# Convolution and MLP block in FP32: fewer idle matmuls ahead of the first group, another split of the last group, one statistics chain for the first two

One core of a Trainium2 chip. The metric is the device time of one execution in microseconds (us), median of several; "slow" states are told apart, and all runs quoted here are of the fast state. The trace and the page come from one profiled execution of each kernel. Its span is 1.7 to 2.0 us shorter than its time. "Clock" is the share of TensorE's full clock that the record shows as granted, as a mean over a run unless a stretch is named.

## The reference

```python
# x: (8, 4224, 192) f32, weight: (8 heads, 7 taps)
w   = softmax(weight, axis=-1)                     # per head
x   = causal depthwise conv over the sequence: sum_k w[h, k] * x_pad[:, s + k, head h]
mu  = mean(x, -1);  var = mean((x - mu)**2, -1)    # moe block, D = 192
xn  = (x - mu) / sqrt(var + 1e-6) * g_ln
out = x + relu(xn @ w_ch1) @ w_ch2                 # 192 -> 768 -> 192
```

## The kernel before

The work is cut into 18 groups of (128 partitions x n tokens), n = 6, 8, 9, 10 for the first sequence and then 16 and 17 by turns; the last is group 17 with 17 tokens. For each group VectorE convolves (`conv`), transposes (`yt`) and takes statistics; TensorE does the up product (`ph`, ScalarE's Relu empties it from PSUM), then the down product, which is either plain (`po`) or made of seven half products instead of eight (`pd`, Strassen's scheme, 7/8 of the columns for some additions on VectorE). The last group does 9 tokens the fast way and 8 the plain way, in two pieces of 4. Cut to what the change touches:

```python
fast = {g: groups[g][2] if g >= 5 else 0 for g in range(NG)}   # tokens by half products
fast[NG - 1] = (J + 1) // 2                                    # J = 17: 9 in the last group
psum = ctx.enter_context(tc.tile_pool(name="ps", bufs=8, space=PSUM))
...
def keep_warm(times):                       # matmuls whose result nobody reads
    idle = psum.tile([P, 512], F32, tag="ps", name="idle")
    for _ in range(times):
        nc.tensor.matmul(idle[:, 0:P], less, copy, start=True, stop=True)
...
def blocks(n):
    half = n if n * C <= 512 else (n + 1) // 2                 # C = 32 columns a token
    return [slice(i, min(i + half, n)) for i in range(0, n, half)]
...
# up(g): for each of 6 chunks f and each block: four PSUM banks, 6 x 4 matmuls, four Relus
# down(g): for each c: one bank, 6 x 4 matmuls
    order = [(c, js) for c in range(NC) for js in blocks(n)]
    if g + 1 == NG:
        order = [(c, slice(j, j + 4)) for j in range(fast[g], n, 4) for c in range(NC)]
...
keep_warm(20)
first_tap(0, heads=(0, PE_HEADS[0])); conv(0, heads=PE_HEADS[0])
centre_w1()                                 # needs the first weights, loaded by DMA
keep_warm(24)
first_tap(1); transpose(0)                  # VectorE: input of group 0
split_words(*words_2); join_words(w2flat, *words_2)   # w2: VectorE and ScalarE (L189)
for g in range(NG):
    up(g)
    ...
    if g < 4: stats(g)                      # bn_stats per token, then 16 small operations
    ...
    if fast[g]: finish_fast(g, *parts)      # additions, 6 transposes
    if g + 1 == NG: add_and_store(g, slice(0, fast[g]))
    down(g); finish(g)                      # per bank a transpose; adds; last store
```

## Time and profile before

| | before |
|---|---|
| median, first 3 runs | 1017.43 us (1017.35 to 1017.55) |
| span of the profiled run | 1015.5 us |
| TensorE busy | 1004.1 us (99%) |
| VectorE busy | 899.1 us (89%) |
| ScalarE busy | 491.9 us (48%) |

TensorE is busy without a hole from the first product of group 0 to the last group, so only the two ends and the number of columns can give anything. The lines that show this, and how to read them, are in the prediction below. PE is TensorE, PEld its weight loads, DVE VectorE, ACT ScalarE; "<-" ahead of a name says what ended an idle time.

### The profile page before, as it was taken

To read this page: it belongs to the slowest core of one execution; us is meant where nothing else is said; L and a number is where in the kernel's file an instruction comes from. 1 tells how busy PE (TensorE), PEld (TensorE's weight loads), DVE (VectorE), ACT (ScalarE), POOL (GpSimd) and SP (SyncE) were. 2 spreads that over 40 slices of the span, in tenths; PEclk is the share of its full clock that TensorE was granted. 3 is DMA by queue.
4 is the path that set the end of the run, shared out by engine and by line. 5 is a ranking of instruction groups with operands and counts; after the bars stand their busy time and mean duration, and the time that the engine had idled before them with its cause. 6 is when DMAs were issued, how large, how long until landed. Compare 5 with 4: busy or idle time off the path is not lost.

```text
span 1015.5 us, 35457 instructions
## 1 busy us (share of the span) xinstructions
PE 1004.1 (99%) x15940; PEld 657.0 (65%) x15940; DVE 899.1 (89%) x1791; ACT 491.9 (48%) x1306; POOL 41.1 (4%) x59
## 2 busy tenths in 40 slices
PE   7999999999999999999999999999999999999997
PEld 6987564348545785458754686556854578545897
DVE  7999798955999999999998999989999999999535
ACT  6445344406445464555536465364644546453450
POOL 1001000000000000000000000000000000000000
PEclk9999999999999999999999999999999999999999
DMA  5233541502323433123333331334232343112031
GB/s 195 100 125 103 160 130 56 161 35 39 89 92 63 157 65 149 34 45 150 64 149 51 117 90 34 148 68 157 39 88 93 64 157 64 65 32 37 2 66 69
DMA packets 12214, 91.45 MB, mean 90 GB/s; under 512 B 1695, under 2 KB 2463, under 8 KB 8222
## 3 DMA queue, kind: packets, MB, share of 16 engines
q1 hardware_dynamic: 6862, 64.91, 16.6%
q0 software_dynamic: 4896, 24.28, 14.3%
q8 instruction: 124, 2.03, 0.8%
q14 instruction: 28, 0.23, 0.1%
q10 hardware_dynamic: 304, 0.00, 0.0%
HBM read 38.95 MB, written 50.23 MB: 88 GB/s over the span
## 4 chain that ended last, share of the span: by engine, by line
PE 98%; DVE 1%; DMA 0%; ACT 0%; issue 0%; DVEq 0%; ACTq 0%
PE ph L444 51%; PE pd L542 35%; PE po L480 11%; PE idle L313 1%; DMA taps<-in_weight_dram 0%; PE pc L273 0%; PE pw L297 0%; PE pw L302 0%; ACT room L266 0%; DVE y L622 0%; PE pm L282 0%; PE pm L285 0%; DVE room L205 0%; DVE room L197 0%; DVE room L194 0%
## 5 line engine op out<-in xcount | busy, mean ns | idle before, releaser
L444 PE MATMUL ph<-yt,w 32*128 32x256 f32 (+4 forms) x7200 | 516.5, 443 | 0.0
L444 PEld LDWEIGHTS ph<-yt,w 32*128 32x128 f32 x7200 | 364.3, 185 | 149.7 <-issue 117.5
L346 DVE SCALAR_TENSOR_TENSOR y<-xg,taps,y 128x384 f32<-128x384 f32 (+5 forms) x852 | 429.1, 582 | 0.0
L456 ACT ACTIVATE ht<-ph 128x288 f32<-128x288 f32 (+4 forms) x600 | 222.7, 457 | 265.7 <-PE ph L444 262.7
L542 PE MATMUL pd<-ht,w 128*32 128x256 f32 (+2 forms) x2808 | 155.9, 378 | 0.0
L542 PE MATMUL pd<-ht,w2sums 128*32 128x256 f32 (+2 forms) x2808 | 153.2, 378 | 0.0
L542 PEld LDWEIGHTS pd<-ht,w 128*32 128x32 f32 x2808 | 89.5, 110 | 64.6 <-issue 6.9
L542 PEld LDWEIGHTS pd<-ht,w2sums 128*32 128x32 f32 x2808 | 90.9, 110 | 59.9
L480 PE MATMUL po<-ht,w 128*32 128x128 f32 (+5 forms) x2016 | 112.5, 383 | 1.2 <-issue 1.2
L547 ACT COPY cs<-pd 128x272 f32<-128x272 f32 (+2 forms) x156 | 58.3, 373 | 109.1 <-PE pd L542 109.1
L509 DVE TENSOR_TENSOR s<-ht 128x1088 f32<-128x1088 f32 (+2 forms) x39 | 47.5, 1219 | 56.8 <-ACT ht L456 56.8
L480 PEld LDWEIGHTS po<-ht,w 128*32 128x32 f32 x2016 | 62.1, 110 | 50.7 <-issue 23.8
L610 ACT ACTIVATE ot<-ot,r 128x192 f32<-128x192 f32 x247 | 93.1, 471 | 0.0
L547 ACT COPY part<-pd 128x272 f32<-128x272 f32 (+2 forms) x117 | 43.5, 372 | 86.2 <-PE pd L542 86.2
L336 ACT ACTIVATE y<-xg,taps 128x384 f32<-128x384 f32 (+5 forms) x142 | 74.1, 591 | 22.7 <-DVE st L370 18.3
L370 DVE BATCH_NORM_STATS2 st<-y 128x6 f32<-128x192 f32 x264 | 69.7, 341 | 0.0
L357 DVE STREAM_TRANSPOSE yt<-y 128x3072 f32<-128x3072 f32 (+5 forms) x18 | 56.0, 3111 | 1.7 <-DVE y L346 1.0
L614 POOL DMA_DIRECT2D out_dram<-ot x34 | 29.5, 883 | 664.6 <-DVE y L346 388.3
L542 PE MATMUL pd<-s,w2sums 128*32 128x272 f32 (+2 forms) x936 | 52.6, 378 | 0.0
L510 DVE TENSOR_TENSOR ht<-ht 128x1088 f32<-128x1088 f32 (+2 forms) x39 | 47.6, 1220 | 2.2
L586 DVE STREAM_TRANSPOSE ot<-cs 128x544 f32<-128x544 f32 (+2 forms) x78 | 47.5, 672 | 0.0
L520 DVE TENSOR_TENSOR ht<-s,ht 128x1088 f32<-128x1088 f32 (+2 forms) x39 | 45.2, 1214 | 1.6 <-PE pd L542 1.6
(76 smaller groups left out, 280.7 us busy)
## 6 DMA issues: line engine op xcount, KB each, us to landing
xg<-in_x_dram SPq DMA_DIRECT2D x7, 2208.0 KB, 12.5
out_dram<-ot POOLq DMA_DIRECT2D x20, 768.0 KB, 6.7
xg<-in_x_dram SPq DMA_DIRECT2D x7, 2112.0 KB, 11.8
out_dram<-y SPq DMA_DIRECT2D x7, 1536.0 KB, 6.0
out_dram<-y SPq DMA_DIRECT2D x6, 1632.0 KB, 6.2
out_dram<-ot POOLq DMA_DIRECT2D x6, 864.0 KB, 7.5
out_dram<-y SPq DMA_DIRECT2D x2, 864.0 KB, 4.2
xg<-in_x_dram SPq DMA_DIRECT2D x1, 1536.0 KB, 8.8
```

Of the source, the lines that this page charges most:

```text
L336: nc.scalar.mul(dst, src, tap)
L346: nc.vector.scalar_tensor_tensor(out=y[g][:, 0:n, cs], in0=t[:, k : k + n, cs], scalar=taps[:, h, k : k + 1], in1=y[g][:, 0:n, cs], op0=AL ...
L357: nc.vector.transpose(yt[g][:, 0:n].rearrange("p j c t -> p (j c t)"), y[g][:, 0:n].rearrange("p j d -> p (j d)"),)
L370: nc.vector.bn_stats(out=st[:, j, :], in_=y[g][:, j, :])
L444: nc.tensor.matmul(ph[q][:, 0:w], w1[rows, c, fs], t[rows, js, c, :], start=(c == 0), stop=(c == NC - 1),)
L456: nc.scalar.activation(dst, src, AF.Relu)
L480: nc.tensor.matmul(bank[C * q : C * q + C, 0:w], w2[:, f, C * c : C * c + C], t[:, f, q, js.start - fast[g] : js.stop - fast[g], :], start ...
L509: nc.vector.tensor_tensor(s1[g][:, f], a[:, 1, 0, f], a[:, 1, 1, f], op=ALU.add)
L510: nc.vector.tensor_tensor(a[:, 1, 0, f], a[:, 0, 0, f], a[:, 1, 0, f], op=ALU.subtract)
L542: nc.tensor.matmul(dst[C * q : C * q + C, 0:w], right[:, f, C * c : C * c + C], left[:, f, q], start=(first and f == 0), stop=(f == FC - 1 ...
L547: nc.scalar.copy(to[:, c], dst[:, 0:w].rearrange("p (j t) -> p j t", t=T))
L610: nc.scalar.mul(ots[g][:, j, :], ots[g][:, j, :], rstd[g][:, j : j + 1])
```

## The change

The intent: let group 0 start sooner, move three tokens of the last group from the plain product to the cheaper half products, finish the last group with fewer instructions and in one piece, and save VectorE one chain of small operations. Core of the diff:

```diff
-    fast[NG - 1] = (J + 1) // 2
+    fast[NG - 1] = J - 5
@@ stats: split into moments(g) (bn_stats) and root(g, n) (the chain)
+        if g == 0:
+            moments(0)
+        elif g == 1:
+            moments(1)
+            root(0, groups[0][2] + groups[1][2])
+            rstd[1] = rstd[0][:, groups[0][2] :]
@@ blocks
-        half = n if n * C <= 512 else (n + 1) // 2
-        return [slice(i, min(i + half, n)) for i in range(0, n, half)]
+        cut = fast[g] if 0 < fast[g] < n else n // 2 if n * C > 512 else 0
+        return [slice(0, cut), slice(cut, n)] if cut else [slice(0, n)]
@@ down
-            order = [(c, slice(j, j + 4)) for j in range(fast[g], n, 4) for c in range(NC)]
+            order = [(c, slice(fast[g], n)) for c in range(NC)]
@@ down_fast, two half products before its end; finish_fast now takes one half
+        if g + 1 == NG:
+            finish_fast(g, 0, cs, part)
@@ head
-    keep_warm(24)
+    keep_warm(12)
```

More of the change, by code (lines that the diff above doesn't have):

```diff
@@ L360, in transpose, with moments, root @@
         )
+    sums = {}
+    def moments(g):
+        n = groups[g][2]
+        if g == 1:
+            sums[g] = sums[0][:, groups[0][2] :]
+        else:
+            sums[g] = spool.tile([P, J, nc.vector.BN_STATS_DIM], F32, tag="st", name=f"st{g}")
+        for j in range(n):
+            nc.vector.bn_stats(out=sums[g][:, j, :], in_=y[g][:, j, :])
     def stats(g):
-        n = groups[g][2]
-        st = spool.tile([P, J, nc.vector.BN_STATS_DIM], F32, tag="st", name=f"st{g}")
+        moments(g)
+        root(g, groups[g][2])
+    def root(g, n):
+        st = sums[g]
         dt = spool.tile([P, J], F32, tag="d", name=f"d{g}")
@@ L368, in stats @@
         d, v, r = dt[:, 0:n], vt[:, 0:n], rt[:, 0:n]
-        for j in range(n):
-            nc.vector.bn_stats(out=st[:, j, :], in_=y[g][:, j, :])
         nc.vector.tensor_tensor(d, st[:, 0:n, 1], st[:, 0:n, 4], op=ALU.subtract)
@@ L407, with blocks @@
     ht = {}
-    def blocks(n):
-        half = n if n * C <= 512 else (n + 1) // 2
-        return [slice(i, min(i + half, n)) for i in range(0, n, half)]
+    def blocks(g):
+        n = groups[g][2]
+        cut = fast[g] if 0 < fast[g] < n else n // 2 if n * C > 512 else 0
+        return [slice(0, cut), slice(cut, n)] if cut else [slice(0, n)]
     def up(g):
@@ L434, in up @@
             fs = slice(f * P, f * P + P)
-            for js in blocks(n):
+            for js in blocks(g):
                 w = (js.stop - js.start) * C
@@ L471, in down @@
         po[g] = []
-        order = [(c, js) for c in range(NC) for js in blocks(n)]
+        order = [(c, js) for c in range(NC) for js in blocks(g)]
         if g + 1 == NG:
-            order = [(c, slice(j, j + 4)) for j in range(fast[g], n, 4) for c in range(NC)]
+            order = [(c, slice(fast[g], n)) for c in range(NC)]
         for c, js in order:
@@ L577, in down_fast, with finish_fast @@
         return cs, part
-    def finish_fast(g, cs, part):
+    def finish_fast(g, half, cs, part):
         n = fast[g]
-        ot = out_tile(g)
-        c21, c22 = cs[:, 0:CH, :, 1], cs[:, CH:NC, :, 1]
-        nc.vector.tensor_tensor(c21, c21, part[:, 1], op=ALU.add)
-        nc.vector.tensor_tensor(c22, c22, part[:, 2], op=ALU.add)
-        for c in range(NC):
+        ot = ots[g] if half else out_tile(g)
+        fresh = cs[:, CH * half : CH * half + CH, :, 1]
+        nc.vector.tensor_tensor(fresh, fresh, part[:, 1 + half], op=ALU.add)
+        for c in range(CH * half, CH * half + CH):
             nc.vector.transpose(
@@ L684 @@
                 store_y(g + 1)
-        if g < 4:
+        if g == 0:
[4 more added lines that the diff above has]
+            rstd[1] = rstd[0][:, groups[0][2] :]
+        elif g < 4:
             stats(g)
@@ L690 @@
         if fast[g]:
-            finish_fast(g, *parts)
+            for half in range(g + 1 == NG, 2):
+                finish_fast(g, half, *parts)
         if g + 1 == NG:
```

## The prediction

> **What bounds the kernel now.** I read the page first, for the bound, then the waits of TensorE, then the two ends in the timeline and in the chain that ended last, because the middle turned out to have no hole in it.
>
> The page's busy row, and its chain by engine:
>
> ```profile
> PE 1004.1 (99%) x15940; PEld 657.0 (65%) x15940; DVE 899.1 (89%) x1791; ACT 491.9 (48%) x1306; POOL 41.1 (4%) x59
> ...
> PE 98%; DVE 1%; DMA 0%; ACT 0%; issue 0%; DVEq 0%; ACTq 0%
> ```
>
> The matrix engine is the bound: 98% of the path that sets the end is its work. The waits of that engine alone (who waited on whom, us in total, times, longest):
>
> ```profile
> PE idle L313 <- POOL room L251: 4.8, 1, 4.8
> PE po L480 <- issue: 1.2, 2, 0.9
> PE pm L282 <- DVE room L205: 0.9, 1, 0.9
> ```
>
> It waits at the very start, and for 1.2 us "issue" in the last down product. From the first product of group 0 (28.86 us) to there it never waits. So a change counts only in three ways: fewer or cheaper TensorE instructions, an earlier start of group 0, or a shorter tail. The start of group 0, in the timeline (start, length, engine, what):
>
> ```profile
> 23.31 5.62 PE L313 MATMUL idle<-room 128*128 128x128 f32 x48
> ...
> 25.69 1.38 DVE L357 STREAM_TRANSPOSE yt<-y 128x1152 f32<-128x1152 f32 x1 [0.51 <-DVE y L346]
> ...
> 28.86 11.98 PE L444 MATMUL ph<-yt,w 32*128 32x192 f32 x288
> ...
> 29.21 1.26 ACT L189 ACTIVATE spare<-spare,low 128x1152 int32<-128x1152 int32 x1 [0.30 <-DVE spare L186]
> ...
> 31.16 1.00 ACT L456 ACTIVATE ht<-ph 128x192 f32<-128x192 f32 x4 [0.69 <-PE ph L444]
> ```
>
> The input of group 0 is transposed at 25.69 + 1.38 = 27.07 us, but the idle matmuls (24 in the program, 48 records, two passes each) hold the engine until 28.86. The tail, in the chain in order of time:
>
> ```profile
> 977.88 15.57 PE pd L542 x504
> 993.45 8.94 PE po L480 x326
> 1002.39 0.88 issue
> 1003.27 3.70 PE po L480 x128
> 1006.97 0.32 issue
> 1007.30 2.38 PE po L480 x77
> ...
> 1012.00 0.33 DVE y L622 x2
> ```
>
> The last group ends with 15.57 us of half products (9 tokens), 17.5 us of plain product (8 tokens, two pieces), then transposes, adds and a store.
>
> **What the Trainium skill says.** "TensorE: Matmul & The Clock Gate", section "Back-to-back issue gap", gives a warm matmul N/2.4 + 2.5 ns. The trace agrees if an FP32 pass counts two cycles a column: 63 sets of four 256-column matmuls took 27.33 us, 433.8 ns a set, two passes of 216.9; the formula at N = 512 gives 215.8. "ScalarE: Activation LUTs", section "What ACT_TABLE_LOAD costs", gives an ACTIVATE 0.833 ns per element; here four Relus of 256 columns take 1.21 us and of 288 columns 1.32 us in the timeline, 0.86 ns a column. "Runtime: NRT & Kernel Launch", section "Instruction fetch mechanics", says an engine's instructions come in blocks of 256 (16 KiB), fetched by DMA and mostly hidden. The trace agrees on the size (the instruction queue has 124 packets in 2.03 MB; between the two "issue" gaps lie 128 matmul and 128 weight-load records) and shows two that are not hidden, while the tail's stores run. The first page's section "Why this matters for your kernels" asks for no idle gap over about 3 us; the change leaves one of 1 us, and the page shows full clock in every slice, although the engine already sits idle for 0.88 us at L282. So I expect no clock loss.
>
> **The change part by part.**
>
> *Idle matmuls, 24 to 12.* 48 records took 23.31 to 28.86, 0.1156 us each. With 24 the engine is free at about 26.1 and then waits for the transposed input, 27.07 + 0.05 (the lag seen from DVE L205's end, 12.30, to the product at 12.35). Group 0 starts at 27.12: 1.74 us earlier. But something takes part back. Eight PSUM banks hold two blocks of four, so the third block needs the first Relus done. ScalarE's queue holds the conversion of w2 (L189) before them; it ends at 30.47 whatever TensorE does, because it waits for VectorE. The first four Relus then end near 31.6 rather than follow the product at 29.4. The third block would start at 27.12 + 2 x 1.985 = 31.1, so about 0.5 us of wait, with weight load 0.6. Net **-1.15 us**. The input of group 1 is ready at 49.09 + 1.78 = 50.87; the product would want it at 52.61 - 1.15 = 51.46, so no wait, but only 0.6 us to spare.
>
> *One statistics chain for groups 0 and 1.* Removes 16 VectorE operations at about 0.18 us spacing, 2.9 us in all (52.44 to 55.36). VectorE is not on the path there: group 2's input is ready at 74.9, used at 84.1. **0 us.**
>
> *Middle groups.* The block cut of the 17-token groups becomes 8 + 9 instead of 9 + 8: the same columns. The order of instructions on each engine shows no other move. **0 us.**
>
> *Last group, up products.* Two blocks of 288 and 256 columns become 384 and 160; the sum is equal, so are the matmul counts. But the 160-column block lasts only 6 sets x 274 ns = 1.64 us, and within it four Relus of 384 columns have to free the banks that the next block takes: 1.32 + 4 x 96 x 0.00086 = 1.65 us, after a lag of 0.3 us (the Relu starts 0.3 us after the next block's first matmul in the trace), plus the last one's overlap. The fourth bank comes free some 0.35 us late, 0.55 with the weight load. There are five such hand-overs. If each costs in full it is 1.75 us or more; if the row groups can run a little apart, a part is absorbed. I take **+1.1 us**.
>
> *Last group, down.* A half product of w columns: 144 columns take 15.57/63 = 247.1 ns a set, 256 take 433.8, so 192 take 327.1 and 63 sets 20.61 us: +5.04. The plain piece: 128 columns take 219 ns a set (banks are released every 1.31 us, six sets), so 160 take 274 and 36 sets 9.86 us, instead of 72 x 219 = 15.78: -5.92. Sum **-0.88 us**. This is the intended saving (three more tokens at 7/8 of the plain cost).
>
> *The fetch gaps.* The engine's end was about 1010.98 = 993.45 + 15.78 + 1.75, so gaps with restart cost 1.75 us, though the waits show 1.2. After the change the plain piece has half the instructions, so a block of 256 lasts 4.4 us instead of 3.5. The program has 48 + 576 = 624 TensorE instructions fewer, which puts the last two block edges 388 and 132 instructions from the end, 6.6 and 2.3 us before it. The big store starts about 4.7 us before the end, so those blocks should be on their way by then. **-1.75 us**, the least certain gain.
>
> *The tail after TensorE.* Half of the fast result is now finished while two half products still run. VectorE's remaining three transposes, then 12 adds at 0.339 us (9 took 3.05), end some 4.7 us before TensorE ends, in time for the plain banks. After the fifth bank come 5 wide adds instead of 4 and 5 narrow ones: 1.55 us behind TensorE instead of 1.35, **+0.2**. The last store is 480 KB instead of 384: from 2.3 us for 384 KB and 4.1 for 864, **+0.36**.
>
> Sum: -1.15 + 1.1 - 0.88 - 1.75 + 0.56 = **-2.1 us**: 1017.43 becomes about 1015.3; I put it at 1015.1, because I think the hand-over more likely smaller than larger.
>
> **The rivals.**
>
> *A. The hand-over wait eats the gain.* Each of the five costs 0.55 us or more and they add up to nearly 3 us, or a fetch gap stays. For it: ScalarE alone releases those banks, with 1.65 us of work in 1.64. Against: four banks are released one by one, three of them in time. It would end at 1016.5 to 1017.5.
>
> *B. All parts go well.* Group 0 starts 1.74 us earlier with nothing taken back, the fetch gaps vanish, the hand-over costs nothing: 1.74 + 0.88 + 1.75 - 0.56 = 3.8, 1013.6. Against: L189's end is fixed by VectorE.
>
> *C. The earlier start is lost later.* VectorE, 89% busy, becomes the limit for some group's input, and the head's gain is waited away there. For it: the 0.6 us to spare at group 1. Against: in the later groups VectorE's work hangs on TensorE's own progress, and before group 17 the input is ready at 942.1, used at 944.6. It would cost 1.15: 1016.3.
>
> *D. VectorE becomes the tail*, with 12 adds and wider transposes. I find 1 us of slack; if a late ScalarE copy uses it up, the end moves by under 1 us.
>
> **Range and chances.** Head -0.7 to -1.74, hand-over 0 to +2.5, fetch -0.5 to -1.75, the rest firm to some 0.3. Not all go one way, so 1013.4 to 1016.8 holds it 8 times in 10. Two per cent is 20 us; the whole of both ends that the change touches is smaller than that, except by a fault. Within 2%: 0.985.
>
> **What would show it.** Right: the idle group has 24 records, group 0 starts near 27.1; a wait of about 0.5 us on ScalarE in its third block; five waits or stretched blocks in the last up stage (33.25 us becomes about 34.3); half products of 20.6 us, plain ones of 9.9 without an "issue" gap; VectorE's last add 1.5 us behind the last product. Wrong: a clock under 1.00 after the gap, an "issue" gap in the plain piece, a wait of TensorE on VectorE at group 1 or 2, or the twelve adds running into the plain banks.

## The result, and the profile after

1014.28 us (1014.06 to 1014.6, 6 runs) against 1017.49 us (1017.35 to 1017.69, 6 runs) of the kernel before on the same chip: ratio 0.9969, 95% interval 0.9956 to 0.9981. Ratios are the mean time of one kernel's fast runs over that of the other's of the same rounds, so not quite the ratio of the medians quoted. The gain is 3.2 us; the prediction's sum had 2.1 and its number 2.3, and the time lies inside its range.

TensorE's waits after, all of them (us in total, times, longest):

```profile
PE idle L313 <- POOL room L251: 4.8, 1, 4.8
PE ph L457 <- DVE yt L357: 1.0, 1, 1.0
PE pm L282 <- DVE room L205: 0.6, 1, 0.6
```

The "issue" wait of the last down product is gone, and there is a new wait of 1.0 us: group 0 now waits for its transposed input and no longer for the idle matmuls. The timeline of the head after the change:

```profile
23.26 2.94 PE L313 MATMUL idle<-room 128*128 128x128 f32 x24
...
25.64 1.38 DVE L357 STREAM_TRANSPOSE yt<-y 128x1152 f32<-128x1152 f32 x1 [0.51 <-DVE y L346]
...
27.16 12.25 PE L457 MATMUL ph<-yt,w 32*128 32x192 f32 x288 [0.96 <-DVE yt L357]
...
29.16 1.26 ACT L189 ACTIVATE spare<-spare,low 128x1152 int32<-128x1152 int32 x1 [0.30 <-DVE spare L186]
30.32 2.01 ACT L469 ACTIVATE ht<-ph 128x192 f32<-128x192 f32 x8
```

The first Relus start when L189 is done, eight in one run with no wait between: that is the part given back. The product of group 0 is listed with 12.25 us against 11.98. And the tail, in the chain that ended last. The up stage of group 17 before:

```profile
944.66 33.21 PE ph L444 x576
```

and all of it after:

```profile
943.23 33.60 PE ph L457 x558
976.83 20.61 PE pd L555 x504
997.44 8.19 PE po L493 x240
...
1008.32 0.49 DVE y L636 x3
```

The stages of both kernels, from the records in the two traces (from the first matmul of a stage to the first of the next; the plain stage to its last matmul):

| us | before | after | difference | predicted |
|---|---|---|---|---|
| first matmul of group 0 | 28.86 | 27.16 | -1.70 | -1.74 |
| its up stage | 11.91 | 12.18 | +0.27 | +0.6 |
| all from there to group 17 | 903.82 | 903.82 | 0 | 0 |
| up stage of group 17 | 33.21 | 33.60 | +0.39 | +1.1 |
| half products | 15.46 | 20.50 | +5.04 | +5.04 |
| plain product | 17.44 | 9.66 | -7.78 | -7.67 |
| last matmul to last add | 1.62 | 1.89 | +0.27 | +0.2 |
| last add to the span's end | 3.21 | 3.49 | +0.28 | +0.36 |
| sum | | | -3.23 | -2.1 |

The sum is the difference of the spans, 1015.54 and 1012.29, to the rounding. The whole middle, 904 us with 17 groups, is the same to 10 ns.

### The profile page after: what moved, and what is told of

Same layout as the page of the kernel before. It is cut to its first block, busy times and chain, and to the rows that moved or that the text cites. A ratio compares the mean times of both kernels' runs of the same rounds, so it can differ in the third digit from the quotient of the medians.

```text
span 1012.3 us, 34807 instructions
## 1 busy us (share of the span) xinstructions
PE 1000.9 (99%) x15628; PEld 648.8 (64%) x15628; DVE 900.4 (89%) x1766; ACT 490.5 (48%) x1306; POOL 41.1 (4%) x59
## 4 chain that ended last, share of the span: by engine, by line
PE 97%; DVE 2%; DMA 0%; ACT 0%; issue 0%; DVEq 0%; ACTq 0%
PE ph L457 51%; PE pd L555 35%; PE po L493 10%; DVE y L346 1%; DMA taps<-in_weight_dram 0%; DVE y L636 0%; ACT room L266 0%; DVE room L197 0%; DVE yt L357 0%; DVE room L194 0%; ACT room L181 0%; DVE ot L653 0%; ACT room L189 0%; DVE room L186 0%; DVE room L180 0%
## 5 line engine op out<-in xcount | busy, mean ns | idle before, releaser
L457 PE MATMUL ph<-yt,w 32*128 32x256 f32 (+6 forms) x7200 | 517.1, 443 | 1.0 <-DVE yt L357 1.0
L469 ACT ACTIVATE ht<-ph 128x256 f32<-128x256 f32 (+6 forms) x600 | 222.7, 457 | 268.9 <-PE ph L457 265.5
L555 PE MATMUL pd<-ht,w 128*32 128x256 f32 (+2 forms) x2808 | 158.0, 382 | 0.0
L555 PE MATMUL pd<-ht,w2sums 128*32 128x256 f32 (+2 forms) x2808 | 155.3, 381 | 0.0
L493 PE MATMUL po<-ht,w 128*32 128x192 f32 (+5 forms) x1728 | 106.0, 406 | 0.0
L493 PEld LDWEIGHTS po<-ht,w 128*32 128x32 f32 x1728 | 55.6, 110 | 49.5 <-issue 22.1
L600 DVE STREAM_TRANSPOSE ot<-cs 128x544 f32<-128x544 f32 (+2 forms) x78 | 50.0, 690 | 2.7 <-ACT cs L560 1.0
```

The source lines that it names most:

```text
L457: nc.tensor.matmul(ph[q][:, 0:w], w1[rows, c, fs], t[rows, js, c, :], start=(c == 0), stop=(c == NC - 1),)
L469: nc.scalar.activation(dst, src, AF.Relu)
L493: nc.tensor.matmul(bank[C * q : C * q + C, 0:w], w2[:, f, C * c : C * c + C], t[:, f, q, js.start - fast[g] : js.stop - fast[g], :], start ...
L555: nc.tensor.matmul(dst[C * q : C * q + C, 0:w], right[:, f, C * c : C * c + C], left[:, f, q], start=(first and f == 0), stop=(f == FC - 1 ...
L600: nc.vector.transpose(ot[:, 0:n, C * c : C * c + C], cs[:, c].rearrange("p j h t -> p j (h t)"))
```

## The experiments

They ran on three other chips, in three lots of four. There the first weights arrive later: the first real matmul (`pm`) starts at 14.2 to 14.5 us instead of 12.3, and the kernel before takes about 1020 us. Many of their runs also show a mean clock of 0.994 to 0.998 instead of 0.999 or 1.000. So beside the medians I give the median of the runs with a clock of 0.999 and above, called "full clock": it compares like with like. For the kernel before this is 1019.93 us on the chip of the first lot (32 of 47 runs), 1019.81 on that of the second (28 of 41) and 1019.52 on that of the third (6 of 14).

### 1. Idle matmuls back to 24

```diff
-    keep_warm(12)
+    keep_warm(24)
```

> The changed kernel with its 12 idle matmuls set back to 24, nothing else. Theory (the idle matmuls held back group 0, and ScalarE's conversion of w2 gives back about 0.35 us): group 0 starts near 28.9 us instead of 27.16, its up stage takes 11.9 us again instead of 12.25, and the time is 1.4 us above the changed kernel, about 1015.7. Rival (an earlier start is lost later, or the whole gain is the tail's): less than 0.4 us above it.

Median 1018.43 us; ratio to before 0.9983 (0.9976 to 0.999). At full clock 1018.34 (14 runs), 1.6 below the kernel before; experiment 4, which has the 12 idle matmuls, is at 1016.25. The head is worth 2.1 us on this chip, not 1.4. In the traces group 0 starts at 31.57 us here and at 29.14 in experiment 8, another chip with the weights as late, and its up stage takes 11.91 against 12.18: 2.43 - 0.27 = 2.16. The mechanism is the one expected; the size depends on when the weights come. The idle matmuls start after the weights' work (26.02 us here, 23.31 on the first chip) but the input of group 0 is ready only 2.0 us later than there (29.07 against 27.07), so 24 of them overrun it by more.

### 2. No idle matmuls ahead of group 0

```diff
-    keep_warm(12)
```

> The changed kernel with no idle matmul ahead of group 0. Theory (after the change the start of group 0 is set by VectorE's transposition, which ends at 27.03 us): group 0 starts at 27.1 to 27.2 again and the time is the changed kernel's, 1014.3 give or take 0.3. Rival (the clock gate closes in the 3.9 us without a matmul[...]): the first products of group 0 take up to twice as long, the recorded clock is lower, and the time is 1.5 to 3 us longer.

Median 1017.72 us (11 runs), none at full clock: 0.995 to 0.998. That is 1.5 us above experiment 4 at full clock. The rival is right. The stretch of group 0's up stage (columns: length, then busy us and count of PE, PEld, DVE, ACT and POOL, the granted clock, the DMA share, GB/s), and the next:

```profile
27.00:42.83 15.83, 13.66 (x293) 13.22 (x296) 14.10 (x29) 11.48 (x35) 0.00 (x0) 0.89 0.37 134
42.83:48.00 5.17, 5.17 (x131) 4.13 (x135) 5.17 (x17) 1.64 (x6) 0.00 (x0) 1.00 0.02 3
```

A mean of 0.89 over 15.83 us is 3.5 us at half clock. The record has one such stretch of 3.41 us here (and one earlier), and the up stage of group 0 took 13.35 us instead of 12.18. That stretch began at 28.96 us, within a wait of 2.2 us ahead of group 0. So the idle matmuls do a job, and 12 are not just "fewer is better".

### 3. The last group's change alone

```diff
-    fast[NG - 1] = (J + 1) // 2
+    fast[NG - 1] = J - 5
@@ and the blocks, the one plain piece and the early half as in the change; 24 idle matmuls, two chains
```

> The kernel before with the change of the last group alone (12 tokens in half products, one plain piece of 5, the first half finished early); 24 idle matmuls and two statistics chains as before. Theory (head and tail add up, the statistics count nothing): 1.8 us below the kernel before, about 1015.7, with no issue gap in the plain piece. Rival (they don't add up, since the earlier head shifts the instruction blocks against the stores): the gaps appear and it is under 1 us below.

Median 1018.55 us, ratio 0.9986 (0.9979 to 0.9993); at full clock 1018.43 (13 runs), 1.5 below before. The up stage, half products and plain product of group 17 take 33.60, 20.50 and 9.66 us, as in the changed kernel, with no issue gap. With the head's 2.1 it makes 3.6 to 3.7, what experiment 4 shows. Head and tail add up.

### 4. Two statistics chains again

```diff
-        if g == 0:
-            moments(0)
-        elif g == 1:
-            moments(1)
-            root(0, groups[0][2] + groups[1][2])
-            rstd[1] = rstd[0][:, groups[0][2] :]
-        elif g < 4:
+        if g < 4:
             stats(g)
```

> The changed kernel with the statistics of groups 0 and 1 in two chains again (16 more VectorE operations, 2.9 us of VectorE time). Theory (VectorE has slack there, TensorE never waits for it after group 0): the changed kernel's time within 0.3 us, 1014.3. Rival (with the head 1.4 us earlier that slack is needed): TensorE waits for VectorE at group 2 and the time is 0.5 to 2.5 us longer.

Median 1016.33 us (5 runs), ratio 0.9964 (0.9951 to 0.9977); at full clock 1016.25 (3 runs). TensorE waits for VectorE nowhere after group 0, and the stretch from group 0's down product to group 17 is 903.82 us, as in every other kernel here. The merged chain is worth nothing.

### 5. Before, with the 8 plain tokens in one piece

```diff
-            order = [(c, slice(j, j + 4)) for j in range(fast[g], n, 4) for c in range(NC)]
+            order = [(c, slice(fast[g], n)) for c in range(NC)]
```

> The kernel before with its plain part of 8 tokens in one piece of 256 columns instead of two of 128: the same columns, half the instructions, so a block of 256 instructions lasts 7 us instead of 3.5. Theory (the two issue gaps are late instruction blocks): no issue gap, the plain stage takes 36 sets x 435 ns = 15.7 us instead of 17.5; the tail behind it grows by about 3.3 us (8 wide and 8 narrow adds instead of 4 and 4: 2.0; 768 KB in the last store instead of 384: 1.4), so the time is about 1.6 us longer than before. Rival (the gaps belong to something else, such as banks not yet released by VectorE): the gaps stay, the stage takes above 17 us, the time is over 3 us longer.

Median 1020.16 us, ratio 1.0004 (0.9996 to 1.0013); at full clock 1019.89 (4 runs), as before. The plain stage takes 15.45 us instead of 17.44 and runs without a gap:

```profile
997.07 15.82 PE L480 MATMUL po<-ht,w 128*32 128x256 f32 x287
```

With the same columns and half the instructions the two gaps are gone: 2.0 us. That the time stands still is the longer tail: last matmul to last add 2.55 us instead of 1.62, from there to the end 4.17 instead of 3.21 (768 KB in the last store). I had expected 1.6 us more; the saving was larger and the tail's growth smaller than I had reckoned. The one piece was a choice between two costs, and only with 5 tokens instead of 8 does it pay.

### 6. The changed kernel, its plain piece cut into 3 and 2

```diff
-            order = [(c, slice(fast[g], n)) for c in range(NC)]
+            order = [(c, js) for js in (slice(fast[g], fast[g] + 3), slice(fast[g] + 3, n)) for c in range(NC)]
```

> The changed kernel with its plain piece of 5 tokens cut into 3 and 2 (96 and 64 columns): the same columns, twice the instructions, so a block of 256 would last 2.7 and 1.8 us. Theory (a block takes some 3 to 3.5 us to arrive, so instruction supply becomes the bound): issue gaps return, the plain stage takes 12 to 14 us instead of 9.8, and the time is 1 to 3 us longer although the tail is shorter by about 1.3 us. Rival (only the store's traffic delays a block): gaps only in the 3 us after the store starts, the stage takes under 11 us, the time is the same or shorter.

Median 1020.04 us (12 runs), ratio 0.9998 (0.9989 to 1.0006); at full clock 1019.03 (3 runs), against 1016.2 of experiment 8 on the same chip. The timeline of TensorE:

```profile
1000.23 7.26 PE L493 MATMUL po<-ht,w 128*32 128x96 f32 x350
1009.06 1.99 PE L493 MATMUL po<-ht,w 128*32 128x64 f32 x128 [1.57 <-issue]
1012.53 1.64 PE L493 MATMUL po<-ht,w 128*32 128x64 f32 x98 [1.48 <-issue]
```

The gaps are back, 128 matmul records (256 instructions with their weight loads) apart, and the stage takes 13.73 us instead of 9.66. The packets of the instruction queue, in the trace: 1006.21 to 1007.77 us, after which TensorE goes on at 1009.06; and 1010.25 to 1011.14, after which it goes on at 1012.53. A block comes into use 1.3 to 1.4 us after its packet. The stores' packets ran from 1006.36 to 1011.62, so the second gap lies at their end; this run does not tell supply from traffic.

### 7. Before, with the store of the fast tokens held back

```diff
         if g + 1 == NG:
-            add_and_store(g, slice(0, fast[g]))
+            add(g, slice(0, fast[g]), slice(0, D))
@@ after finish(g) of the last group
+            nc.sync.dma_start(out=<the 9 tokens>, in_=y[g][:, 0 : fast[g]])
```

> The kernel before with the store of the 9 fast tokens held back until all plain tokens are stored. Theory A (a block of instructions comes late because that store's packets fill the DMA engines): the gap of 0.88 us at 1002.4 us goes, the second at 1007.0, behind the store of the first plain piece, may stay; TensorE ends 1.0 to 1.7 us earlier, the program some 1 us later because the store now lies in the tail. Theory B (blocks of 3.5 us are too short for the supply with no store about as well): both gaps stay, and TensorE ends where it did.

Median 1020.8 us, ratio 1.0008 (1.0002 to 1.0015); at full clock 1020.62 (12 runs), 0.8 longer. The plain stage takes 16.27 us instead of 17.44. The timeline of the weight loads, first two lines of the kernel before and then this run:

```profile
1003.27 3.43 PEld L480 LDWEIGHTS po<-ht,w 128*32 128x32 f32 x128 [1.15 <-issue]
...
1007.29 3.41 PEld L480 LDWEIGHTS po<-ht,w 128*32 128x32 f32 x122 [0.59 <-issue]
```

```profile
996.78 8.98 PEld L480 LDWEIGHTS po<-ht,w 128*32 128x32 f32 x326
1006.01 3.43 PEld L480 LDWEIGHTS po<-ht,w 128*32 128x32 f32 x128 [0.26 <-issue]
1009.76 3.41 PEld L480 LDWEIGHTS po<-ht,w 128*32 128x32 f32 x122 [0.32 <-issue]
```

The edges lie at the same places (326, 128 and 122 records), but the waits shrink from 1.15 and 0.59 us (TensorE's own: 0.88 and 0.32) to 0.26 and 0.32, and TensorE has none. So both are true: without the traffic the supply just about keeps up with 256 instructions in 3.5 us, and the store of 864 KB makes a block 0.9 us late. Of the 2.0 us that experiment 5 regained, 1.2 belong to the place of that store. The packets in the two traces say the same. In the kernel before, the instruction packets of the two late blocks run from 1000.97 to 1001.84 and from 1004.69 to 1005.82 us. Each begins when the packets of a store end, at 1000.97 (864 KB) and at 1004.69 (384 KB), and TensorE goes on 1.4 to 1.5 us after the end of the packet. In this run the packet ahead of the second edge begins at 1007.16, just before those of the 384 KB store (1007.30), and isn't held up.

### 8. Both halves of the fast result finished late

```diff
-        if g + 1 == NG:
-            finish_fast(g, 0, cs, part)
@@
-            for half in range(g + 1 == NG, 2):
+            for half in range(2):
```

> The changed kernel with both halves of the fast result finished after the last half product, as before the change. Theory (the early half takes 2.2 us of VectorE work out of the stretch behind the half products, which has 1 to 1.5 us to spare): the twelve adds end near 1004.8 instead of 1002.5, the plain banks' transpositions queue up behind them, the last add ends 0.3 to 0.6 us later, and the time is 0.3 to 1 us longer. Rival (VectorE has slack enough): the same time within 0.2 us.

Median 1016.68 us (6 runs), ratio 0.997 (0.9958 to 0.9983); at full clock 1016.2 (3 runs), 3.6 below before, as experiment 4 is on its chip (3.7). The rival is right: the last matmul to the last add takes 1.89 us in both. The reason stands in the timeline of the changed kernel, where the three last transposes wait for ScalarE's copies one by one:

```profile
995.91 0.58 DVE L600 STREAM_TRANSPOSE ot<-cs 128x384 f32<-128x384 f32 x1 [0.22 <-ACT cs L560]
...
996.88 0.58 DVE L600 STREAM_TRANSPOSE ot<-cs 128x384 f32<-128x384 f32 x1 [0.40 <-ACT cs L560]
...
997.86 0.58 DVE L600 STREAM_TRANSPOSE ot<-cs 128x384 f32<-128x384 f32 x1 [0.40 <-ACT cs L560]
998.48 4.04 DVE L636 SCALAR_TENSOR_TENSOR y<-ot,r,y 128x192 f32<-128x192 f32 x12
```

The twelve adds start 1.04 us after the plain product begins, with the early half or without (1000.45 against 999.42 in experiment 8, 998.48 against 997.44 here). Work taken away from in front of a wait is worth nothing.

### 9. Idle matmuls 28 and 8 instead of 20 and 12

```diff
-    keep_warm(20)
+    keep_warm(28)
@@
-    keep_warm(12)
+    keep_warm(8)
```

> The changed kernel with 28 idle matmuls at the very start instead of 20, and 8 ahead of group 0 instead of 12. On the two other chips the first weights came 2 us later than on the first, TensorE waited 2.7 to 3.3 us ahead of its first real product, and in a third of the runs the record shows a stretch of 3.4 us at half clock in the head, which cost about 1.1 us. Theory (that wait closes the clock gate, and the second lot of idle matmuls has room to spare): the share of runs with a clock under 0.999 falls to nearly none, the best runs are as fast as the changed kernel's within 0.3 us, the median is 0 to 1 us better. Rival (the half clock has nothing to do with that wait): the share stays at a third.

Median 1016.23 us (1016.2 to 1016.41, 4 runs), all at full clock; ratio 0.996 (0.9945 to 0.9975). In the same lot 3 of 5 runs of the changed kernel and 8 of 14 of the kernel before were below it. TensorE's wait ahead of its first real product is 1.4 us instead of 3.2 (experiment 11), and the stretch at half clock is gone. Experiment 12, with the same idle matmuls, is at full clock in its four runs too. The head of experiment 12 and then of experiment 11, columns as in experiment 2 (0.90 against 1.00 is the clock):

```profile
14.00:31.00 17.00, 14.91 (x140) 11.55 (x144) 16.20 (x47) 13.19 (x36) 0.00 (x0) 1.00 0.58 201
14.00:31.00 17.00, 16.62 (x132) 12.94 (x136) 16.17 (x47) 12.31 (x35) 0.00 (x0) 0.90 0.60 205
```

With few runs, this is a strong hint rather than a proof; over all profiled runs the picture is the same:

| profiled run | wait ahead of `pm`, us | half clock in the head |
|---|---|---|
| before, changed (first chip), experiments 9, 10, 12 | 0.5 to 1.9 | no |
| 1, 8 | 2.7 | no |
| 7, 3, 4, 6, 11, 2, 5 | 2.9 to 3.3 | yes, 3.41 us, from 14.9 to 15.7 us on, just after the wait |

The length of the wait isn't the whole of it. In all seven runs of the last row the half clock begins 6.83 us, twice 3.41, after the full clock began. In the 3.41 us just before it, TensorE's matmul records fill 14 to 37% of the time. In the stretch at the same place the others have 43% (experiment 10), 46% (1 and 8), 59% (9), 68% (12) and 98% or more (first chip). So it also matters where a wait falls: in experiments 1 and 8 the full clock began at 9.1 to 9.3 us instead of 8.0 to 8.9, and 2.7 us of waiting were split between two stretches. No single share explains every case: the second half clock of experiment 2 follows a stretch with 50%.

### 10. 13 tokens in half products

```diff
-    fast[NG - 1] = J - 5
+    fast[NG - 1] = J - 4
```

> The changed kernel with 13 tokens in half products and 4 plain. Columns save 0.29 us more, the tail 0.9 us (4 wide and narrow adds instead of 5, 384 KB instead of 480 in the last store). But the short up block is 128 columns, 1.31 us, against four Relus of 416 columns, 1.8 us with the lag. Theory A (row groups can run apart by no more than one pass, so each of the five hand-overs costs what is over that): the last up stage takes 34.5 to 36 us instead of 33.6 and the time is 0 to 1.5 us above the changed kernel's. Theory B (only the first hand-over costs, as in the changed kernel's trace): the stage takes under 34.3 us and the time is 0.6 to 1.2 us below. In both, plain blocks of 128 columns bring the 3.5 us per 256 instructions back, so an issue gap may return.

Median 1017.98 us, ratio 0.9978 (0.9968 to 0.9987): 1.8 us above the changed kernel at full clock (1017.9 of 6 runs, 1016.1 of 2). Theory A: the last up stage takes 35.02 us instead of 33.60. ScalarE's Relus there, and in the changed kernel, each line one chunk (eight Relus in a row):

```profile
955.45 2.60 ACT L469 ACTIVATE ht<-ph 128x416 f32<-128x416 f32 x8 [3.18 <-PE ph L457]
...
961.32 2.42 ACT L469 ACTIVATE ht<-ph 128x416 f32<-128x416 f32 x8 [1.92 <-PE ph L457]
...
966.93 2.60 ACT L469 ACTIVATE ht<-ph 128x416 f32<-128x416 f32 x8 [1.83 <-PE ph L457]
```

```profile
952.83 2.67 ACT L469 ACTIVATE ht<-ph 128x384 f32<-128x384 f32 x8 [2.98 <-PE ph L457]
...
958.33 2.68 ACT L469 ACTIVATE ht<-ph 128x384 f32<-128x384 f32 x8 [1.46 <-PE ph L457]
...
963.83 2.67 ACT L469 ACTIVATE ht<-ph 128x384 f32<-128x384 f32 x8 [1.46 <-PE ph L457]
```

A chunk without waiting is 33.21/6, 5.5 us. With 12 tokens the chunks follow at exactly 5.50 us once the first hand-over is past; with 13 they take 5.87 and 5.61 by turns. The matmul records suggest why. With 12, the four matmuls of a set start within 21 ns of each other before the first hand-over. After it the fourth (in order of start) comes 236 ns behind the third in every chunk's passes of 384 columns, to the end, and such a pass lasts 322 ns. The late bank delays one row group (each of the four matmuls of a set reads another 32 of the 128 partitions), once, and the others do not wait. With 13 the largest step within a set is 265 to 287 ns of the 349 ns of a pass; it lies by turns between the first and second start and between the third and fourth, and time is lost at every hand-over. That one pass is the limit of this slack is my reading of the two; no run varies the lateness finely. No gap from instructions came back. Of the rest, the columns and the tail, the trace shows that the store of 13 tokens now runs into the last one: their packets form one stretch from 1009.01 to 1014.42 us.

### 11. The changed kernel again

> The changed kernel itself once more, as the yardstick of these runs on this chip. If the chip loads the first weights as late as the two of the earlier experiments did: group 0 starts near 29.1 us, and it is about 3.7 us below the kernel before in the runs without a half clock, since the 24 idle matmuls cost 2.1 us there. If it loads them as early as the first chip: 3.2 us below.

Median 1017.14 us (5 runs), ratio 0.9965 (0.9952 to 0.9978); at full clock 1016.1 (2 runs), 3.4 below the kernel before. Its profiled run is one with a half clock: group 0 starts at 29.94 us.

### 12. A version with a shorter tail

```diff
+    keep_warm(28) ... keep_warm(8)
@@ finish, last group
+            if left == NC - 2: add(g, js, slice(0, D - 2 * C))
+            if left == NC - 1: add_narrow(g, js, slice(D - 2 * C, D - C))
+            if left == NC:
+                for part in (first 3 tokens, last 2):
+                    add_narrow(g, part, slice(D - C, D)); store_part(g, part)
+    def add_narrow(g, js, ds):     # one product with rstd broadcast, one addition
```

> The changed kernel with the idle matmuls at 28 and 8, and a shorter tail: the wide add covers four banks and comes after the fourth, the fifth and sixth banks are added by one multiplication with the broadcast scale and one addition instead of an operation a token, and the last store goes out in two parts of 3 and 2 tokens. Theory: 0.26 us from the wide add moved, about 0.4 from the narrow adds, up to 1.1 from the smaller last store (288 and 192 KB; landing 2.3 us for 384 KB, 4.1 for 864), so 1 to 1.8 us below the changed kernel, and few runs at half clock. Rival (the store's fixed time, or the second issue, sets the end): 0.6 us below.

Median 1015.61 us (1015.55 to 1015.89, 4 runs), all at full clock; ratio 0.9954 (0.9939 to 0.9969), the fastest of all. It is 0.6 below experiment 9, which has the same head. The rival is right about the size. The last operations of VectorE:

```profile
1008.42 0.33 DVE L645 TENSOR_TENSOR ot<-ot,r 128x160 f32<-128x160 f32 x1
1008.78 0.32 DVE L646 TENSOR_TENSOR y<-y,ot 128x160 f32<-128x160 f32 x1
1009.60 0.35 DVE L667 STREAM_TRANSPOSE ot<-po 128x160 f32<-128x160 f32 x1 [0.49 <-PE po L493]
```

VectorE now waits for the last bank, so the wide add is off the path: the last transpose starts 0.37 us after the start of the last matmul instead of 0.61 in experiment 9 (0.24 us, for 0.26 reckoned). The narrow adds gained nothing: four operations for the two parts run from 1009.98 to 1010.93, 0.95 us, against 0.90 for five. The smaller last store gained 0.4, not 1.1 (last add to the span's end 3.07 us instead of 3.49).

## Why the prediction was right

**Head: mechanism right, two sizes off by a little.** Group 0 started at 27.16 us (27.12 predicted), held by the transposed input, and ScalarE's L189 took a part back. The term that was mis-sized is that part: 0.27 us for 0.6. The first Relus did wait for L189, but they ran back to back behind it, and the third block as a whole was not held: it starts 3.98 us after the first, against 4.00 before. In the records only its fourth matmul comes late, 120 ns behind the third instead of 7; the four stay apart from there, and the 0.27 us appear once, where the down product begins. It is what the last group shows below. The predicted slack of group 1 held: no wait of TensorE on VectorE after group 0. Experiments 1 and 4 show the head and the rest to be separate.

**Statistics and middle: right.** Nothing, in experiment 4 and in the 903.82 us.

**Up stage of the last group: the hand-over was mis-sized.** I named the right wait, the fourth bank 0.35 us late, and then put it at +1.1 us as a mean between paying it five times and sharing it out. It was paid once: +0.39. The trace shows how the rest was taken up: one of the four starts stays 236 ns behind. This is the largest error, 0.7 of the 1.1 us by which the sum was short. Rival A, that the hand-overs eat the gain, was wrong for 384 columns; experiment 10 shows that with 416 against 128 columns it is real (+1.4 us for the one token more), so the change stops one token short of it.

**Half products and plain piece: right to 0.1 us.** 20.61 us in the chain for 20.61 predicted, and 9.66 from first to last matmul for 9.86 to its end. Both fetch gaps went, as predicted. Experiments 5, 6 and 7 show what they are: instruction blocks that come late, because the pieces of 128 columns use up 256 instructions in 3.5 us and because their packets start only when those of a store end (1000.97 and 1004.69 us, experiment 7). In the change both were relieved at once (4.4 us a block, and the store falls after the fetches); the reckoning of where the block edges fall cannot be told apart from the lower demand, and stays open.

**Tail: right as a sum (+0.55 for +0.56).** But the early finish of the first half, which I counted as what lets VectorE be in time, is worth nothing (experiment 8): the second half hangs on ScalarE's copies anyway. My expectation for that run was wrong for the same reason. Rival D did not come: VectorE waited for the plain banks.

**Rival C** (the head's gain lost later) is excluded by the equal middle. **Rival B** came nearest in size, 3.8 for 3.2, since it left the hand-over out.

**What I did not foresee** is that the size depends on the chip. On the three others the weights come 2 us later. The head is worth 2.1 us instead of 1.4 on the one where it was measured alone, and a stretch at half clock costs 1.1 us in part of the runs (1018.34 against 1019.48 us by median in experiment 1). The first chip's six runs of the changed kernel had none. I had expected no clock loss after 12 idle matmuls, which held; experiment 2 shows that without them it is lost.

## What to carry to other kernels

Where one engine is busy throughout, read the two ends record by record: half of this gain was two gaps of an engine that the page calls 99% busy, and they went with fewer and longer instructions and a store that comes after the fetches, not with less arithmetic. Idle matmuls have to cover a wait, no more: too many hold back the work, none costs the clock, and the right number depends on when the data come. A buffer that comes late to one of four matmuls side by side may cost once and not each time; measure one hand-over before multiplying it.

## What the Trainium skill lacked or had wrong

- "Runtime: NRT & Kernel Launch", section "Instruction fetch mechanics", calls the cost of a block edge mostly hidden. In the kernel before two edges cost 2.0 us of a plain stage of 17.4 us (experiment 5), and in experiment 6 two gaps of 1.57 and 1.48 us follow one another. It gives no rate; here 256 instructions of TensorE in 3.5 us were just supplied without other traffic (waits of 0.26 and 0.32 us at the edges, experiment 7) and not beside a store of 864 KB (1.15 us), and a block came into use 1.3 to 1.5 us after its packet (experiment 6 and the kernel before).
- "TensorE: Matmul & The Clock Gate", section "Why this matters for your kernels", asks for no gap over about 3 us. Here a wait of 2.9 us ahead of the first real product was followed by 3.41 us at half clock (experiment 7), 2.7 us was not in two profiled runs (1 and 8), and in experiment 2 such a stretch began within a wait of 2.2 us ahead of group 0. The stretch has the window's length that this page gives in section "What's actually happening"; that a wait shorter than a window can bring it is what the page lacks. In the seven runs TensorE was 14 to 37% busy in the 3.41 us before, not idle throughout (experiment 9).
- None of the pages read says how far the four row groups of a set may run apart: 236 ns of a 322 ns pass cost 0.39 us once and nothing more in the changed kernel, and in experiment 10 265 to 287 of 349 ns came with lost time at each hand-over.
- None of the pages read says that the same loads land 2 us later on another chip: the first real product started at 12.3 us on one chip and at 14.2 to 14.5 us on three.
